# A cross network's first layer: the remainder of x0 in two loads, and the layer as x0 * (psum + b + 1)

## The chip, the core and the metric

The kernel runs on one core of one Trainium2 chip. The metric is the device time of one execution in microseconds (us), the median of several runs; lower is better. A profiled execution gives, beside it, a trace of every engine: TensorE (PE in the profile, its weight loads PEld), VectorE (DVE), ScalarE (ACT), GpSimd (POOL) and SyncE (SP), which here only issues DMAs. ACTq and SPq are the issuing sequencers of those engines.

## What is computed

```
B, F, D, L = 4096, 26, 16, 6
Din = min(F * D, 1024)            # 416
# x0: (4096, 416), ws: (6, 416, 416), bs: (6, 416), all bfloat16
x = x0
for l in range(6):
    x = x0 * (x @ ws[l] + bs[l]) + x
return x
```

In the first layer x is x0 itself, so that layer is x0 * (x0 @ w + b) + x0, which is the same as x0 * (x0 @ w + b + 1).

## The kernel before, in words

The work is held transposed: the 416 features lie on partitions and the 4096 rows of the batch are columns. The features are cut into NK = 3 blocks of 128 and a remainder of R = 32. The columns are cut into NS = 2 halves (s) of NG = 4 groups (g) of CW = 512. XM[0] holds x0's three blocks, XM[1] and XM[2] alternate as the layers' results; XR[0] to XR[2] hold the remainder, with group g of a half on partitions 32g to 32g+31. XRd is a second copy of x0's remainder with the two pairs of groups swapped (partitions 64 to 127 hold groups 0 and 1), so that two row matmuls can use different parts of the array.

*Loads.* `load_x0t(s, g)` (L74) loads one group of x0 with a transposing DMA, 393 KB, issued by SP. The remainder's 32 columns come as 64-byte pieces: for the first half by four DMAs on ACT's queue into xrig (L78), for the second by one on SP into xrem (L83), which POOL then regroups into xrig (L134). `load_wm` loads a layer's weights for the three blocks, `load_wr0` (L87) the 32 remaining weight rows of layer 0, which ACT (twice) and POOL (once) copy to the other three groups of 32 partitions (L107 to L112). SP's issues stand in the order in which they are written: x0's groups 0 and 1, WR of layer 0, groups 2 and 3, group 0 of the second half, xrem, groups 1 to 3 of the second half, then the other layers' weights and row copies for the last layer.

*Fillers.* While the first loads are under way TensorE runs matmuls on a constant tile (`pe_filler`, L139): two of 256 columns, then nine of 512. Then it transposes the biases (`bias_setup`, L146), which DVE copies to bM and bR.

*First layer* (`first_layer`, L208), half by half. `full` (L211) is three 128 x 512 matmuls, one per feature block, for one output block m and one group; `row` (L217) adds the remainder's 32 rows to two groups; `mm_rem` (L191) makes the remainder's own output. PSUM has four buffers of two banks that are taken in turn, so a tile of two groups can start only when the fourth tile before it has been read out. `x0_rem` (L155) transposes xrig with four TensorE transposes into PSUM and has DVE copy the result to XR[0] (one copy of 128 partitions) and XRd (two of 64). In the first half the order on TensorE is: group 0 for all m, x0_rem for the first half, group 1 for all m, rows, groups 2 and 3 of m = 0, 1, 2, rows, mm_rem, x0_rem for the second half. `ew_main` (L162) follows for each tile: ACT adds the bias while it reads PSUM (L165), DVE multiplies with x0 (L166), DVE adds the old x (L169). `ew_rem` (L171) does so for the remainder.

*Layers 1 to 4* (L282) work in the same transposed form with matmuls cut into four column tiles (L181), and the last layer is made row by row (L315 onward) with the result sent out from there.

The order of instructions on an engine is a scheduler's, starting from the order in which they are written; `keep_in_program_order` pins one. A tile's readers and writers on different engines are kept apart by semaphores that the framework puts in; two engines that read one PSUM tile are also put one behind the other.

Of the kernel before, what the change touches and what calls it, by code (L numbers as in the profile page):

```python
# [9 lines left out]
ACT = mybir.ActivationFunctionType  # L10
ALU = mybir.AluOpType
BF16 = mybir.dt.bfloat16
FP32 = mybir.dt.float32
# [3 lines left out]
def kernel(  # L17
# [7 lines left out]
    nc = tc.nc  # L25
    B, D = x0.shape
    L = ws.shape[0]
    P = 128
    NK = 3
    R = D - NK * P  # L30
    assert R == 32 and B == 4096 and D == 416 and L >= 2
    NS = 2
    NG = 4
    CW = 512
# [5 lines left out]
    big = ctx.enter_context(tc.tile_pool(name="big", bufs=1))  # L40
    tpool = ctx.enter_context(tc.tile_pool(name="tpool", bufs=6))
# [3 lines left out]
    x0_v = x0.rearrange("(bt p) d -> p bt d", p=P)  # L45
# [13 lines left out]
    X0rows = big.tile([P, NBT, D], BF16)  # L59
    XLrows = big.tile([P, NBT, D], BF16)  # L60
    scrR = [big.tile([P, 4, P], BF16, name=f"scrR{s}") for s in range(NS)]
    xrem = big.tile([P, 16, R], BF16)
    xrig = big.tile([P, NS, 4, P], BF16)
    XRd = big.tile([P, NS * CW], BF16)
    XM = [big.tile([P, NK, B], BF16, name=f"XM{i}") for i in range(3)]
    XR = [big.tile([P, NS * CW], BF16, name=f"XR{i}") for i in range(3)]
# [1 line left out]
    def col0(s, g):  # L68
        return SW * s + CW * g
# [4 lines left out]
    def load_x0t(s, g):  # L74
        c0 = col0(s, g)
        nc.sync.dma_start_transpose(out=XM[0][:, :, c0:c0 + CW], in_=x0[c0:c0 + CW, 0:NK * P])  # L76

    def load_xrem0():  # L78
        with nc.allow_non_contiguous_dma(reason="64B row segments"):
            for i in range(4):  # L80
                nc.scalar.dma_start(xrig[:, 0, i, :].rearrange("p (g r) -> p g r", g=NG), x0_v[:, i:16:4, NK * P:D])

    def load_xrem1():  # L83
        with nc.allow_non_contiguous_dma(reason="64B row segments"):
            nc.sync.dma_start(xrem[:], x0_v[:, 16:32, NK * P:D])

    def load_wr0():  # L87
        nc.sync.dma_start(WR[0:R, 0, :], ws[0, NK * P:D, :])

    def load_wr(eng, g, l0, l1):  # L90
        eng.dma_start(WR[32 * g:32 * g + 32, l0:l1, :], ws[l0:l1, NK * P:D, :].rearrange("l r n -> r l n"))
# [8 lines left out]
    load_x0t(0, 0)  # L100
    load_wm(nc.scalar, 0)
    nc.scalar.dma_start(bsb[:], bs[:, :])
    load_x0t(0, 1)
    load_xrem0()
    load_wr0()
    nc.scalar.activation(dz[:, 1:2], dz[:, 0:1], ACT.Identity, bias=dz[:, 0:1], scale=1.0)  # L106
    for g in range(1, NG):  # L107
        dst, src = WR[32 * g:32 * g + 32, 0, :], WR[0:R, 0, :]
# [3 lines left out]
            nc.gpsimd.tensor_copy(dst, src)  # L112
    for g in range(2, NG):
        load_x0t(0, g)
    load_x0t(1, 0)
    load_xrem1()
    for g in range(1, NG):
        load_x0t(1, g)
    load_wm(nc.sync, 1)
    for g in range(NG):  # L120
# [10 lines left out]
            nc.gpsimd.tensor_copy(WD[32 * g:32 * g + 32, l0:l1, g, :], WR[32 * g:32 * g + 32, l0:l1, NK * P:D])  # L131

    fill_wd(0, 1)
    nc.gpsimd.tensor_copy(xrig[:, 1].rearrange("p i (g r) -> p i g r", g=NG), xrem[:].rearrange("p (g i) r -> p i g r", g=NG))  # L134
    fill_wd(1, L)

    wps = psum.tile([P, CW], FP32, tag="ps", name="wps")
# [1 line left out]
    def pe_filler(n, cols):  # L139
        for i in range(n):  # L140
            nc.tensor.matmul(wps[:, 0:cols], lhsT=warm[:, 0:P], rhs=warm[:, 0:cols], start=True, stop=True)  # L141

    pe_filler(2, 2 * P)
    pe_filler(8, CW)

    def bias_setup():  # L146
        pb = psum.tile([P, 4, 8], BF16, tag="ps", name="pb")
        for m in range(NK):
            nc.tensor.transpose(pb[:, m, 0:L], bsb[0:L, 128 * m:128 * m + 128], ident[0:L, 0:L])
        for g in range(NG):  # L150
            nc.tensor.transpose(pb[32 * g:32 * g + 32, 3, 0:L], bsb[0:L, NK * P:D], ident[0:L, 0:L], tile_position=(0, 32 * g))  # L151
        nc.vector.tensor_copy(bM[:], pb[:, 0:NK, 0:L])  # L152
        nc.vector.tensor_copy(bR[:], pb[:, 3, 0:L])

    def x0_rem(s, tpr):  # L155
        for i in range(4):
            nc.tensor.transpose(tpr[:, 128 * i:128 * i + 128], xrig[:, s, i, :], ident[:])  # L157
        for dst, src in ((slice(0, P), slice(0, P)), (slice(64, P), slice(0, 64)), (slice(0, 64), slice(64, P))):
            to = XR[0] if dst == src else XRd
            nc.vector.tensor_copy(to[dst, CW * s:CW * s + CW], tpr[src])  # L160

    def ew_main(l, s, m, h, pt, cur, nxt, pin=False):  # L162
        c0 = col0(s, 2 * h)
        t = tpool.tile([P, 2 * CW], BF16, name="t")
        nc.scalar.activation(t[:], pt[:].rearrange("p a b -> p (a b)"), ACT.Identity, bias=bM[:, m, l:l + 1], scale=1.0)  # L165
        prod = nc.vector.tensor_tensor(out=t[:], in0=t[:], in1=XM[0][:, m, c0:c0 + 2 * CW], op=ALU.mult)  # L166
        if pin:
            tc.keep_in_program_order(prod)
        nc.vector.tensor_tensor(out=nxt[:, m, c0:c0 + 2 * CW], in0=t[:], in1=cur[:, m, c0:c0 + 2 * CW], op=ALU.add)  # L169

    def ew_rem(l, s, pr, curR, nxtR):  # L171
# [34 lines left out]
                                    in_=nxt[:, k, SW * s:SW * s + SW])  # L206

    def first_layer(s):  # L208
        cur, curR, nxt, nxtR = XM[0], XR[0], XM[1], XR[1]

        def full(pt, m, h, gl, after_row):  # L211
            c0 = col0(s, 2 * h + gl)
            for k in range(NK):
                nc.tensor.matmul(pt[:, gl, :], lhsT=WM[:, 0, k, 128 * m:128 * m + 128], rhs=cur[:, k, c0:c0 + CW],  # L214
                                 start=(k == 0 and not after_row), stop=(k == NK - 1 and after_row))

        def row(pt, m, h, opens):  # L217
            for gl in range(2):
                rg = 32 * ((2 * h + gl) ^ (2 if m == 1 else 0))
                src = XRd if m == 1 else curR  # L220
                nc.tensor.matmul(pt[:, gl, :], lhsT=WR[rg:rg + 32, 0, 128 * m:128 * m + 128],  # L221
                                 rhs=src[rg:rg + 32, CW * s:CW * s + CW],
                                 start=opens, stop=not opens, tile_position=(rg, 0))

        def ph(m):
            return psum.tile([P, 2, CW], FP32, tag="ps", name=f"ph{m}")

        pa = [ph(m) for m in range(NK)]
        if s == 0:
            for m in range(NK):  # L230
                full(pa[m], m, 0, 0, False)
            tp0 = psum.tile([P, CW], BF16, tag="ps", name="tpr")
            x0_rem(0, tp0[:])
            for m in range(NK):
                full(pa[m], m, 0, 1, False)
        else:
            for m in range(NK):
                for gl in range(2):
                    full(pa[m], m, 0, gl, False)
        pb = [ph(0)]  # L240
        row(pa[0], 0, 0, False)
        row(pb[0], 0, 1, True)
        row(pa[2], 2, 0, False)
        row(pa[1], 1, 0, False)
        for m in range(NK):
            ew_main(0, s, m, 0, pa[m], cur, nxt)
        for m in range(NK):
            if m:
                pb.append(ph(m))
            for gl in range(2):  # L250
                full(pb[m], m, 1, gl, m == 0)
        row(pb[1], 1, 1, False)
        row(pb[2], 2, 1, False)
        pr = psum.tile([P, 2, CW], FP32, tag="ps", name="pr")
        mm_rem(0, s, pr[:, 0, :], cur, curR)
        if s == 0:
            x0_rem(1, pr[:, 1, :].bitcast(BF16)[:, 0:CW])
        for m in range(NK):
            ew_main(0, s, m, 1, pb[m], cur, nxt, pin=(s == 0))
        ew_rem(0, s, pr[:, 0, :], curR, nxtR)  # L260

    bias_setup()
    pe_filler(1, CW)
# [51 lines left out]
    l = LL  # L315
# [97 lines left out]
```

## Time and profile before

| | |
|---|---|
| device time, median of 3 runs | 130.6 us (130.56 to 130.76) |
| span of the profiled execution (first to last instruction) | 128.9 us |
| median less span | 1.7 us |
| busy: PE, DVE, ACT, POOL | 123.1, 107.1, 86.9, 5.9 us |
| first full matmul of the first layer (L214) starts | 5.84 us |
| first matmul of layer 1 (L181) starts | 26.73 us |
| DMA engines | in nine tenths or more of slices 2 to 12 of 40 |

The profiled execution's own device time is not given apart from its span; the runs' median stands beside it. A matmul in the trace is pipelined: 379 ns is the length of one, but the next can start 216 ns behind it, so TensorE's progress is read from starts, not from lengths. The chain of waits follows the end back to what released each step; an engine that is not on it is idle without cost. In a line of groups the numbers behind the bar are busy time and the mean of one, then the idle time ahead of the group with what ended it.

### The profile page before, as it was taken

What the parts mean: (1) busy time and instruction counts of PE and PEld (TensorE: products, weight loads), DVE (VectorE), ACT (ScalarE), POOL (GpSimd) and SP (SyncE); (2) the same over time, 40 slices, a digit from 0 to 9 for tenths busy, and PEclk for the clock granted to TensorE, in tenths of its full rate; (3) what the DMA queues carried; (4) which work ended last, traced back from release to release, by engine and by line L of the source; (5) the groups of instructions that cost most, each with busy time, mean ns of one, the idle gap of its engine ahead of it and who ended that gap; (6) DMA issues with size and microseconds to landing.
All of it is one profiled execution on the core that took longest, in us unless ns stands there. A gap on an engine that the chain in (4) does not pass through costs nothing.

```text
span 128.9 us, 3973 instructions
## 1 busy us (share of the span) xinstructions
PE 123.1 (96%) x1690; PEld 54.9 (43%) x1690; DVE 107.1 (83%) x197; ACT 86.9 (67%) x99; POOL 5.9 (5%) x18
## 2 busy tenths in 40 slices
PE   6999999999999999999999999999999999999960
PEld 2343443354444444444444444444444445445420
DVE  1032979999999898989898989898989899898991
ACT  0426783987848577848668848668847896569670
POOL 4022200600000000000000000000000000000000
PEclk9999999999999999999999999999999999999999
DMA  3999999999990000000000000000297999995754
GB/s 106 237 203 217 170 158 260 247 328 333 336 299 11 5 0 8 0 0 5 0 5 0 5 0 5 0 5 0 42 166 164 123 219 178 187 323 188 231 179 139
DMA packets 42102, 16.37 MB, mean 127 GB/s; under 512 B 30906, under 2 KB 42084, under 8 KB 42084
## 3 DMA queue, kind: packets, MB, share of 16 engines
q1 hardware_dynamic: 39416, 15.56, 54.6%
q10 hardware_dynamic: 2668, 0.56, 2.3%
q8 instruction: 13, 0.21, 0.7%
q14 instruction: 5, 0.04, 0.1%
HBM read 6.15 MB, written 3.41 MB: 74 GB/s over the span
## 4 chain that ended last, share of the span: by engine, by line
PE 80%; DMA 8%; DVE 5%; issue 2%; SPq 1%; ACT 1%; DVEq 0%
PE pt L181 49%; PE ph L214 9%; DMA XM<-in_x_dram 8%; PE py L327 8%; PE pt L187 5%; PE pr L198 5%; DVE t L355 3%; DVE o L344 2%; PE pr L193 2%; SPq L76 1%; PE py L333 1%; PE ph L221 1%; PE py L336 1%; ACT t L354 1%; PE pr L157 0%
## 5 line engine op out<-in xcount | busy, mean ns | idle before, releaser
L181 PE MATMUL pt<-XM,WM 128*32 128x512 bf16 x1152 | 65.2, 379 | 0.0
L165 ACT ACTIVATE t<-pt,bM 128x1024 bf16<-128x1024 f32 x48 | 49.6, 1115 | 18.3 <-PE pt L187 18.3
L166 DVE TENSOR_TENSOR t<-t,XM 128x1024 bf16<-128x1024 bf16 x60 | 41.4, 690 | 5.3 <-ACT t L165 5.3
L169 DVE TENSOR_TENSOR XM<-t,XM 128x1024 bf16<-128x1024 bf16 x60 | 41.8, 696 | 3.4
L181 PEld LDWEIGHTS <-WM 128*32 128x32 bf16 x1152 | 29.7, 97 | 33.8 <-issue 5.1
L354 ACT CAST t<-py 128x416 bf16<-128x416 f32 (+1 forms) x23 | 14.8, 642 | 4.8 <-PE py L327 2.1
L327 PE MATMUL py<-WM,XM 128*128 128x416 bf16 x96 | 17.7, 340 | 0.0
L214 PE MATMUL ph<-XM,WM 128*128 128x512 bf16 x72 | 16.5, 379 | 0.1
L165 ACT ACTIVATE t<-ph,bM 128x1024 bf16<-128x1024 f32 x12 | 12.5, 1114 | 4.4 <-PE ph L221 4.4
L327 PEld LDWEIGHTS <-XM 128*128 128x128 bf16 x96 | 9.0, 98 | 8.5 <-issue 1.4
L355 DVE TENSOR_TENSOR t<-t,X0rows 128x416 bf16<-128x416 bf16 (+1 forms) x23 | 10.4, 454 | 1.2 <-ACT t L354 1.2
L214 PEld LDWEIGHTS <-WM 128*128 128x128 bf16 x72 | 6.8, 98 | 8.6 <-issue 1.3
L344 DVE TENSOR_TENSOR o<-t,XLrows 128x416 bf16<-128x416 bf16 (+1 forms) x23 | 10.3, 451 | 0.0
L173 ACT ACTIVATE t<-pr,bR 128x512 bf16<-128x512 f32 x10 | 6.4, 684 | 2.7 <-PE pr L198 2.1
L198 PE MATMUL pr<-XM,WM 128*32 128x512 bf16 x120 | 8.2, 379 | 0.0
L187 PE MATMUL pt<-XR,WR 32*128 32x512 bf16 x96 | 7.3, 379 | 0.0
L141 PE MATMUL wps<-warm 128*128 128x512 bf16 (+1 forms) x11 | 4.4, 593 | 1.2 <-DVE warm L94 1.2
L175 DVE TENSOR_TENSOR XR<-t,XR 128x512 bf16<-128x512 bf16 x10 | 4.2, 423 | 0.7
L198 PEld LDWEIGHTS <-WM 128*32 128x32 bf16 x120 | 3.2, 97 | 3.1
L106 ACT ACT_TABLE_LOAD x1 | 1.3, 1283 | 4.3 <-DMA WM<-in_ws_dram 4.3
L174 DVE TENSOR_TENSOR t<-t,XR 128x512 bf16<-128x512 bf16 x10 | 4.2, 418 | 0.0
L152 DVE CAST bM<-pb 128x18 f32<-128x18 bf16 x1 | 0.2, 177 | 4.6 <-PE pb L151 4.6
(39 smaller groups left out, 33.6 us busy)
## 6 DMA issues: line engine op xcount, KB each, us to landing
X0rows<-in_x_dram SPq DMA_DIRECT2D x4, 832.0 KB, 11.6
out_dram<-o SPq DMA_DIRECT2D x9, 208.0 KB, 2.4
WM<-in_ws_dram SPq DMA_DIRECT2D x5, 312.0 KB
out_dram<-o SPq DMA_DIRECT2D x13, 104.0 KB, 1.7
WR<-in_ws_dram SPq DMA_DIRECT2D x4, 130.0 KB, 4.1
WM<-in_ws_dram ACTq DMA_DIRECT2D x1, 312.0 KB
XM<-in_x_dram SPq DMA_TRANSPOSE x8, 4.9
xrig<-in_x_dram ACTq DMA_DIRECT2D x4, 32.0 KB, 4.1
```

The source lines that it names most:

```text
L165: nc.scalar.activation(t[:], pt[:].rearrange("p a b -> p (a b)"), ACT.Identity, bias=bM[:, m, l:l + 1], scale=1.0)
L166: prod = nc.vector.tensor_tensor(out=t[:], in0=t[:], in1=XM[0][:, m, c0:c0 + 2 * CW], op=ALU.mult)
L169: nc.vector.tensor_tensor(out=nxt[:, m, c0:c0 + 2 * CW], in0=t[:], in1=cur[:, m, c0:c0 + 2 * CW], op=ALU.add)
L173: nc.scalar.activation(tr[:, 0:CW], pr, ACT.Identity, bias=bR[:, l:l + 1], scale=1.0)
L181: nc.tensor.matmul(pts[g // 2][32 * q:32 * q + 32, g % 2, :], lhsT=WM[:, l, k, 128 * m + 32 * q:128 * m + 32 * q + 32], rhs=cur[:, k, c0:c ...
L187: nc.tensor.matmul(pts[g // 2][:, g % 2, :], lhsT=WR[32 * g:32 * g + 32, l, 128 * m:128 * m + 128], rhs=curR[32 * g:32 * g + 32, CW * s:CW ...
L198: nc.tensor.matmul(pr[32 * g:32 * g + 32, :], lhsT=WM[:, l, k, NK * P:D], rhs=cur[:, k, c0:c0 + CW], start=False, stop=(k == NK - 1), tile ...
L214: nc.tensor.matmul(pt[:, gl, :], lhsT=WM[:, 0, k, 128 * m:128 * m + 128], rhs=cur[:, k, c0:c0 + CW], start=(k == 0 and not after_row), sto ...
L327: nc.tensor.matmul(py[:, 0:D], lhsT=cur[:, k, q_cols(q, g)], rhs=WM[:, l, k, :], start=((not closes) and k == 0), stop=(closes and k == NK ...
L344: tc.keep_in_program_order(nc.vector.tensor_tensor(out=o, in0=t, in1=xl, op=ALU.add))
L354: nc.scalar.copy(tv, src)
L355: tc.keep_in_program_order(nc.vector.tensor_tensor(out=tv, in0=tv, in1=X0rows[:, b, :], op=ALU.mult))
```

## The change

The remainder of the first half is loaded in two parts (a half's groups 0 and 1, then 2 and 3), all by SP; the four DMAs on ACT's queue go and WR of layer 0 takes their place. Each part has two TensorE transposes and four copies, two by ACT (to XR[0]) and two by DVE (to XRd). The second half's remainder comes in four DMAs straight into xrig, so POOL no longer regroups, and its transposes move from the end of the first half into the second. Groups are worked one at a time. The first layer is x0 * (psum + b + 1): bM and bR get 1.0 added for layer 0, block m = 1 is done by one DVE instruction that reads PSUM, blocks 0 and 2 by ACT and one DVE multiplication, and the addition of x0 is gone. One filler less runs.

```diff
-    xrem = big.tile([P, 16, R], BF16)
-    xrig = big.tile([P, NS, 4, P], BF16)
+    xrh = big.tile([P, 2, 4, 2, R], BF16)
+    xrig = big.tile([P, 4, P], BF16)
...
-    def load_xrem0():
+    def load_xrem0(h):
+        with nc.allow_non_contiguous_dma(reason="64B row segments"):
+            for g in range(2):
+                b0 = 4 * (2 * h + g)
+                nc.sync.dma_start(xrh[:, h, :, g, :], x0_v[:, b0:b0 + 4, NK * P:D])
+
+    def load_xrem1():
         with nc.allow_non_contiguous_dma(reason="64B row segments"):
             for i in range(4):
-                nc.scalar.dma_start(xrig[:, 0, i, :].rearrange("p (g r) -> p g r", g=NG), x0_v[:, i:16:4, NK * P:D])
...
+                nc.sync.dma_start(xrig[:, i, :].rearrange("p (g r) -> p g r", g=NG), x0_v[:, 16 + i:32:4, NK * P:D])
...
     nc.scalar.dma_start(bsb[:], bs[:, :])
+    load_wr0()
     load_x0t(0, 1)
-    load_xrem0()
-    load_wr0()
+    load_xrem0(0)
...
     for g in range(2, NG):
         load_x0t(0, g)
-    load_x0t(1, 0)
+    load_xrem0(1)
+    for g in range(2):
+        load_x0t(1, g)
     load_xrem1()
-    for g in range(1, NG):
+    for g in range(2, NG):
         load_x0t(1, g)
...
-    nc.gpsimd.tensor_copy(xrig[:, 1].rearrange("p i (g r) -> p i g r", g=NG), xrem[:].rearrange("p (g i) r -> p i g r", g=NG))
...
-    pe_filler(8, CW)
+    pe_filler(7, CW)
...
+        nc.vector.tensor_scalar_add(bM[:, :, 0:1], bM[:, :, 0:1], 1.0)
+        nc.vector.tensor_scalar_add(bR[:, 0:1], bR[:, 0:1], 1.0)
...
+    def x0_rem0(h, tp):
+        for j in range(2):
+            nc.tensor.transpose(tp[:, P * j:P * j + P], xrh[:, h, 2 * j:2 * j + 2].rearrange("p i g r -> p (i g r)"), ident[:])
+        for i in range(2):
+            src = tp[64 * i:64 * i + 64, 0:2 * P].rearrange("p (j c) -> p j c", j=2)
+            for to, at, put in ((XR[0], 64 * h, nc.scalar.copy), (XRd, 64 - 64 * h, nc.vector.tensor_copy)):
+                pin(put(to[at:at + 64, 0:CW].rearrange("p (j i c) -> p i j c", j=2, i=2)[:, i], src))
+
+    def x0_rem1(tp):
+        for i in range(4):
+            nc.tensor.transpose(tp[:, P * i:P * i + P], xrig[:, i, :], ident[:])
+        pin(nc.vector.tensor_copy(XR[0][:, CW:2 * CW], tp))
+        pin(nc.scalar.copy(XRd[64:P, CW:2 * CW], tp[0:64]))
+        pin(nc.vector.tensor_copy(XRd[0:64, CW:2 * CW], tp[64:P]))
+
+    def ew_first(s, m, h, pt, on_dve):
+        c0 = col0(s, 2 * h)
+        src, x, b = pt[:].rearrange("p a b -> p (a b)"), XM[0][:, m, c0:c0 + 2 * CW], bM[:, m, 0:1]
+        nxt = XM[1][:, m, c0:c0 + 2 * CW]
+        if on_dve:
+            pin(nc.vector.scalar_tensor_tensor(out=nxt, in0=src, scalar=b, in1=x, op0=ALU.add, op1=ALU.mult))
+            return
+        t = tpool.tile([P, 2 * CW], BF16, name="t")
+        pin(nc.scalar.activation(t[:], src, ACT.Identity, bias=b, scale=1.0))
+        pin(nc.vector.tensor_tensor(out=nxt, in0=t[:], in1=x, op=ALU.mult))
...
         pa = [ph(f"pa{m}") for m in range(NK)]
+        for m in range(NK):
+            full(pa[m], m, 0)
+        full(pa[0], 0, 1)
+        full(pa[1], 1, 1)
+        pb = [ph("pb0")]
         if s == 0:
+            x0_rem0(0, as_bf16(pb[0][:, 0, :]))
         else:
+            x0_rem1(as_bf16(pb[0][:, 1, :]))
+        full(pa[2], 2, 1)
+        row(pa[0], 0, 0)
+        row(pa[1], 1, 0)
+        row(pa[2], 2, 0)
+        if s == 1:
+            row(pb[0], 0, 1, True)
+        for m in (1, 0, 2):
+            ew_first(s, m, 0, pa[m], m == 1)
+        full(pb[0], 0, 2, s == 1)
+        pb += [ph("pb1"), ph("pb2")]
+        full(pb[1], 1, 2)
+        full(pb[2], 2, 2)
+        pr = ph("pr")
+        if s == 0:
+            x0_rem0(1, as_bf16(pr[:, 1, :]))
         for m in range(NK):
+            full(pb[m], m, 3, s == 1 and m == 0)
+        if s == 0:
+            row(pb[0], 0, 1)
+        row(pb[1], 1, 1)
+        row(pb[2], 2, 1)
         mm_rem(0, s, pr[:, 0, :], cur, curR)
+        for m in (1, 0, 2):
+            ew_first(s, m, 1, pb[m], m == 1)
+        ew_first_rem(s, pr[:, 0, :])
```

## Prediction

> **What bounds the kernel now.** I read the page first, then the chain of waits in order of time, then TensorE's timeline in the head, then the groups by shape for prices. The page's chain says who sets the end, and the chain in order of time says where that begins:
>
> ```profile
> span 128.9 us, 3973 instructions
> PE 80%; DMA 8%; DVE 5%; issue 2%; SPq 1%; ACT 1%; DVEq 0%
> ```
>
> ```profile
> 0.74 4.86 DMA XM<-in_x_dram
> 5.61 1.44 SPq L76
> 7.10 5.00 DMA XM<-in_x_dram
> 12.14 3.40 PE ph L214 x15
> ...
> 26.90 2.59 PE pt L181 x48
> ```
>
> Loads set the pace until 12.14 us; from there to 115.8 us the chain is TensorE matmuls without a break, and the last ten microseconds are the drain of the results. So DVE and ACT work taken out of the first layer is worth nothing by itself: only TensorE stalls in the head count, and every one that is added is paid in full, since no idle TensorE time follows that could take it up. TensorE's timeline of the head (start, length, instructions) shows the stalls of today:
>
> ```profile
> 4.57 1.06 PE L141 MATMUL wps<-warm 128*128 128x512 bf16 x2
> 5.84 2.12 PE L214 MATMUL ph<-XM,WM 128*128 128x512 bf16 x9
> 7.80 0.81 PE L157 MATMUL tpr<-ident,xrig 128*128 128x128 bf16 x4
> 8.62 2.10 PE L214 MATMUL ph<-XM,WM 128*128 128x512 bf16 x9
> 10.66 0.60 PE L221 MATMUL ph<-XR,WR 32*128 32x512 bf16 x6
> ...
> 17.01 4.05 PE L214 MATMUL ph<-XM,WM 128*128 128x512 bf16 x18
> ```
>
> ```profile
> 11.20 1.32 PE L214 MATMUL ph<-XM,WM 128*128 128x512 bf16 x4
> ```
>
> A full matmul takes 379 ns but starts every 0.216 us (18 of them in the chain's 3.88 us from 17.18). Nine that start at 5.84 are issued by 7.78; the next nine start at 8.62. Between lie four transposes that cost 0.055 each when fed (0.22 from 16.78 to 17.01), so 0.62 is a stall. Nine from 8.62 end at 10.56 and the rows of L221 start at 10.66: 0.1. Four matmuls from 11.20 that take 1.32 instead of 1.03 hold a wait of 0.29 for the fourth column group.
>
> **Why 8.62.** The second transposed load is the slow one: issued at 2.16, and the longest of L76's "DMA to landing" is 6.4 us, so it lands near 8.6.
>
> ```profile
> 2.16 2.56 SPq L76 DMA_TRANSPOSE XM<-in_x_dram  x1
> DMA to landing us min/median/max: 4.3/4.9/6.4
> ```
>
> Its packets share the 16 DMA engines with 2048 packets of 64 bytes (the four xrig loads). The first load landed at 5.60.
>
> **What goes.** (a) One filler less (0.43 us) ends the fillers at 5.0, so the bias transposes run before the first load lands at 5.60; full work can start at about 5.65 instead of 5.84: -0.2. (b) The four xrig loads leave the ACT queue. In the trace they put about 1.1 us of DMA-engine time among the second load's packets; without them it should land between 7.0 and 7.6, about when nine matmuls from 5.65 end (7.59): -0.62. (c) WR's first load moves from SP to ACT's queue, behind bsb; its two ACT copies (0.54 each) then run before ACT has anything else to do: -0.1. (d) The fourth group is needed only after nine matmuls of the third, near 13.5, where it lands near 12.1 today; on SP the two xrh issues (0.4 to 0.6 each, from xrig and xrem) stand where WR's stood, and g2 no longer waits for g0's landing: -0.29. Together -1.2. The transposes stay eight in all.
>
> **What comes.** T is the start of the two new transposes: 5.65 + 15 x 0.216 = 8.9.
>
> (e) The copies of the first half's remainder. Today three DVE copies of 0.42 lie under nine matmuls (1.94 us). In the change the cover is three matmuls of pa2, 0.65. The order of instructions shows four copies in a strict relay: ACT, DVE, ACT, DVE, each waiting for the one before, because both engines read one PSUM tile. Rows for the prices:
>
> ```profile
> L173 ACT ACTIVATE t<-pr,bR 128x512 bf16<-128x512 f32 x2 | 1.4, 687 | 0.6 <-DVE XRd L160 0.6
> L165 ACT ACTIVATE t<-ph,bM 128x1024 bf16<-128x1024 f32 x12 | 12.5, 1114 | 4.4 <-PE ph L221 4.4
> L160 DVE COPY XRd<-tpr 64x512 bf16<-64x512 bf16 x2 | 0.8, 422 | 0.0
> L152 DVE CAST bM<-pb 128x18 f32<-128x18 bf16 x1 | 0.2, 177 | 4.6 <-PE pb L151 4.6
> ```
>
> ACT: 1114 - 687 = 427 ns for 512 more elements, so some 0.26 fixed and 0.44 to 0.47 for 256 elements; I take 0.44. DVE: between 0.18 (18 elements) and 0.42 (512), so 0.28 for 256. Hand-overs in this trace are 0.04 (ACT to DVE) to 0.09 (DVE to ACT). From T: second transpose done 0.27, start 0.30, ACT 0.74, DVE 1.07, ACT 1.59, rows of pa0 at 1.65; second DVE copy done 1.92, rows of pa1 at 1.98. TensorE is free at 0.11 + 0.65 = 0.76 and works 0.13 between the two: stall 1.1. Bounds: with every copy at its fixed part (0.25, 0.15) and no hand-over 0.2; with 0.69 and 0.42 it is 1.9.
>
> The Trainium skill's PSUM page ("PSUM — Partial Sum Buffer", section "PSUM bank collisions raise a hardware error") says that ScalarE and VectorE must not read one bank in the same 32-partition quadrant at once, so such reads have to be put one behind the other. By it the relay can't be shortened by luck; no run here shows a collision. Without the rule one would count only the longer engine, about 0.9, and get a stall of 0.6.
>
> (f) pb1 takes pa0's PSUM buffer. pa0's rows start at T+1.65; ACT starts 0.43 behind a first row (21.00 to 21.43 in the trace), so 2.08, and with 1.11 the buffer is free at 3.25. TensorE gets there at 1.98 + 0.3 + 0.65 = 2.93: stall 0.3 (0.2 to 0.45). pa1's fused DVE instruction on PSUM has no row; between one bf16 pass (0.69) and two (1.4) it ends by 3.85, and pb2 needs the buffer at 3.9: nothing. (g) In the second half pa0 needs pb0's buffer: pb0's rows at X, free at X+0.43+1.11+0.06 = X+1.6; TensorE arrives after six rows (0.43) and the remainder (0.98) at X+1.4: 0.2 (0 to 0.3). (h) In the second half xrig's transposes move under three matmuls as well. DVE copy 0.42, then ACT's of XRd: 0.38 + 0.03 + 0.42 + 0.05 + 0.69 + 0.06 = 1.63 after the first transpose; TensorE is there at 0.22 + 0.65 + 0.2 = 1.1: 0.55 (0 to 0.55). Today POOL's regrouping and all three DVE copies were hidden. The xrh1 relay lies under nine matmuls and costs nothing; without that cover it would be another 1.9.
>
> Loads: xrh1, s1's groups and four xrig issues instead of one xrem keep SP some 2 to 3 us longer, so layer 1's WM, issued at 17.97 and landed near 22.3 today, lands near 25 and is needed near 27.5. Hidden by about 2 us. The multiply-only form takes 12 adds of 0.69 off DVE, and the two bias adds are tiny: off the chain.
>
> **Sum.** 1.1 + 0.3 + 0.2 + 0.55 = 2.15 against 1.2: +0.95, span 129.85. The runs' median, 130.6, lies 1.7 above the profiled span; with the same surround the forecast is 131.55. With all low ends the net is about -0.4, with all high ends +2.0.
>
> **Rivals.** *Short copies* (faster): if each relay copy takes only its fixed part, with no hand-over, (e) is 0.2, (h) 0, (f) 0.4, (g) 0.2: 0.8 against 1.2 gives 130.2. It turns once relay copies average under about 0.2. For it: no row here has a 256-element PSUM copy; against it: ACT's slope of 0.83 ns an element in two rows. Chance 0.11, and 0.06 for ending within 0.2% (0.26 us, about what a measurement can tell) on the way there.
>
> *Late xrh* (slower still): xrig's landings took a median 4.1 us and xrem's 4.3 from issue. xrh's second load is issued near 5.3; at 4.4 it lands at 9.7 instead of before 8.9, and the transposes stall TensorE 0.8 more: 132.35. Against it: xrem waited behind a transposed load, here too, but this one should have drained by 6.2. Chance 0.12.
>
> *Slow clock*: fillers start every 0.43 us, first-layer matmuls every 0.216; the slow step lasted from 1.19 to at least 5.43 (the page's granted clock has a 9 in every slice, the first too, so only the step tells). With the fillers ending at 5.0 the run is broken for some 0.5 us; if the slow step then lasted another 4.2 us from 5.65, ten matmuls would be done in place of nineteen: +2.1, 133.6. For: the same fillers led straight to the fast step. Against: the gap is short. Chance 0.05. The Trainium skill ("TensorE: Matmul & The Clock Gate", Part 1) has the gate judged in free-running windows of 3.4 us, so a missed window would cost about 1.7; the trace's two steps agree with its two clocks.
>
> **How the numbers follow.** Forecast (net +0.3 to +1.6) 0.66; the rivals 0.11 + 0.06, 0.12, 0.05. Range 130.5 to 132.5: it leaves out short copies at their best, the slow clock and the far ends of (e). Faster 0.11, same 0.06, slower 0.83.
>
> **What would show it.** (a, b) first full matmul near 5.65, ninth followed within 0.1 by the tenth. (e) a gap of about 1.1 between pa2's second-group matmuls and pa1's rows, with ACT, DVE, ACT, DVE end to end in it. (f) 0.3 before pb1. (g, h) 0.2 and 0.5 in the second half; layer 1 starting near 27.7 instead of 26.7. If layer 1 starts before 26.7 the prediction is wrong; if the tenth matmul waits past 8.0, (b) is.

## The result, and the profile after

The changed kernel takes 132.41 us (median of 4 runs, 131.93 to 132.63) against 130.68 for the kernel before in the same session (4 runs, 130.56 to 131.12): a ratio of 1.0121, 95% interval 1.0088 to 1.0154. It is slower by 1.2%, 1.6 us by the ratio. The forecast was 131.55 with a range of 130.5 to 132.5: the direction held, and the time lies at the range's upper end.

The profiled execution took 132.42. Its span and its shares by engine, from the page of after:

```profile
span 130.6 us, 3961 instructions
PE 82%; DVE 6%; DMA 4%; ACT 3%; issue 2%; DVEq 0%
```

Loads give up half of their share of the chain (8% to 4%) and ACT gains 2: the first layer now waits for copies instead of loads. The chain of waits of after, in order of time (start, length, what):

```profile
0.73 4.89 DMA XM<-in_x_dram
...
5.66 3.81 PE pa L245 x15
9.47 0.12 PE pb L165 x2
...
9.62 0.37 ACT XR L169
...
10.02 0.29 DVE XRd L169
...
10.34 0.38 ACT XR L169
...
10.76 0.41 PE pa L252 x2
...
28.28 2.59 PE pt L212 x48
```

The loads leave the chain at 5.6 us, where those of before held it until 12.1 (the head, in what follows, is everything ahead of layer 1). In their place stands the relay: the transposes end at 9.59, ACT copies, DVE copies, ACT copies, and 1.2 us later the rows of L252 start. TensorE's timeline of after (start, length, instructions, idle before) shows what that costs and where it comes again:

```profile
9.42 0.81 PE L245 MATMUL pa<-XM,WM 128*128 128x512 bf16 x3
10.76 0.39 PE L252 MATMUL pa<-XR,WR 32*128 32x512 bf16 x2 [0.52 <-ACT XR L169]
...
20.84 0.81 PE L245 MATMUL pa<-XM,WM 128*128 128x512 bf16 x3
21.59 0.60 PE L252 MATMUL pa<-XR,WR 32*128 32x512 bf16 x3
22.13 0.39 PE L252 MATMUL pa<-XRd,WR 32*128 32x512 bf16 x2
...
22.59 0.39 PE L252 MATMUL pb<-XR,WR 32*128 32x512 bf16 x2
```

Three matmuls are issued in 0.65 us, so TensorE is free at 10.06, but it starts the rows at 10.76. In the second half it is free at 21.49 and is done with its eight rows at 22.91; eight rows that are fed take 0.54 (the chain of before). Layer 1 starts at 28.11 instead of 26.73: 1.38 us of the profiled span's 1.62 (128.93 to 130.55).

**The other 0.25 us** lies behind the last instruction that computes. Both kernels end with ACT issuing the last output; it lands 1.73 us later in before and 1.74 in after. Then the end differs. SP waits for the DMA semaphores one after another. In before, the last output's is the last of these waits; in after it is the first of five, and the other four follow after it has landed, 0.06 each. The groups of SP's last line (instructions, duration in ns min/median/max), in before:

```profile
L408 SPq EVENT_SEMAPHORE  x7: 17/28/28, 126.4 to 128.9; - x7
```

and in after, where one wait takes the whole landing and the rest stand behind it:

```profile
L444 SPq EVENT_SEMAPHORE  x7: 17/28/1677, 127.8 to 130.5; - x7
```

From the last issue to the end it is 2.57 us before and 2.82 after. Before has 64 DMA issues, after 67.

### The profile page after: what moved, and what is told of

It is laid out like the page before. It is cut to its first block, busy times and chain, and to the rows that moved or that the text cites. A ratio compares the mean times of both kernels' runs of the same rounds, so it can differ in the third digit from the quotient of the medians.

```text
span 130.6 us, 3961 instructions
## 1 busy us (share of the span) xinstructions
PE 123.9 (95%) x1689; PEld 55.3 (42%) x1689; DVE 100.4 (77%) x185; ACT 84.8 (65%) x100; POOL 4.1 (3%) x17
## 4 chain that ended last, share of the span: by engine, by line
PE 82%; DVE 6%; DMA 4%; ACT 3%; issue 2%; DVEq 0%
PE pt L212 49%; PE py L363 8%; PE pb L245 6%; PE pa L245 6%; PE pt L218 5%; PE pr L229 5%; DMA XM<-in_x_dram 4%; DVE t L391 3%; DVE o L380 2%; PE pr L224 2%; PE pb L252 1%; PE py L369 1%; ACT t L186 1%; PE py L372 1%; ACT t L390 1%
## 5 line engine op out<-in xcount | busy, mean ns | idle before, releaser
L199 DVE TENSOR_TENSOR t<-t,XM 128x1024 bf16<-128x1024 bf16 x48 | 32.9, 686 | 5.8 <-ACT t L198 5.8
L200 DVE TENSOR_TENSOR XM<-t,XM 128x1024 bf16<-128x1024 bf16 x48 | 33.2, 692 | 3.1
L245 PE MATMUL pa<-XM,WM 128*128 128x512 bf16 x36 | 8.8, 393 | 0.2 <-DMA XM<-in_x_dram 0.2
L245 PE MATMUL pb<-XM,WM 128*128 128x512 bf16 x36 | 8.4, 380 | 0.1
L186 ACT ACTIVATE t<-pb,bM 128x1024 bf16<-128x1024 f32 x4 | 4.3, 1112 | 3.3 <-PE pb L252 1.8
L204 ACT ACTIVATE t<-pr,bR 128x512 bf16<-128x512 f32 x8 | 5.1, 683 | 2.1 <-PE pr L229 2.1
L187 DVE TENSOR_TENSOR XM<-t,XM 128x1024 bf16<-128x1024 bf16 x8 | 5.2, 684 | 0.2 <-ACT t L186 0.2
L183 DVE SCALAR_TENSOR_TENSOR XM<-pb,bM,XM 128x1024 bf16<-128x1024 f32 x2 | 2.6, 1284 | 3.2 <-PE pb L252 3.2
L186 ACT ACTIVATE t<-pa,bM 128x1024 bf16<-128x1024 f32 x4 | 4.2, 1110 | 0.5 <-PE pa L252 0.5
```

Source lines behind the costliest of these rows:

```text
L186: pin(nc.scalar.activation(t[:], src, ACT.Identity, bias=b, scale=1.0))
L245: nc.tensor.matmul(pt[:, g % 2, :], lhsT=WM[:, 0, k, 128 * m:128 * m + 128], rhs=cur[:, k, c0:c0 + CW], start=(k == 0 and not after_row), ...
```

## The experiments

One table for all twelve. The ratio is to runs of the kernel before on the same chip in the same session. "Profiled" is the profiled execution's own time; layer 1's start and the tail (last output's issue to the end) are read from it, so a profile that lies off its median has to be read with that.

| kernel | median us | ratio, 95% interval | profiled | layer 1 starts | tail |
|---|---|---|---|---|---|
| before | 130.68 | | | 26.73 | 2.57 |
| after | 132.41 | 1.0121 (1.0088 to 1.0154) | 132.42 | 28.11 | 2.82 |
| e1_filler | 132.32 | 1.0117 (1.0086 to 1.0147) | 132.44 | 28.09 | 2.82 |
| e2_all_dve | 131.98 | 1.0093 (1.0064 to 1.0123) | 131.93 | 27.70 | 2.81 |
| e3_cover | 132.39 | 1.0114 (1.0073 to 1.0154) | 132.52 | 28.20 | 2.83 |
| e4_half2 | 131.88 | 1.0081 (1.0049 to 1.0112) | 132.41 | 28.07 | 2.81 |
| e5_evac | 132.43 | 1.0109 (1.0085 to 1.0134) | 132.26 | 27.95 | 2.82 |
| e6_form | 134.71 | 1.0282 (1.0254 to 1.0310) | 134.74 | 30.29 | 3.01 |
| e8_xrh_act | 132.68 | 1.0128 (1.0100 to 1.0156) | 133.03 | 28.76 | 2.83 |
| c1_combined | 131.66 | 1.0054 (1.0034 to 1.0075) | 131.97 | 27.82 | 2.74 |
| e9_before_form | 130.90 | 1.0006 (0.9984 to 1.0029) | 130.54 | 26.55 | 2.57 |
| e10_relay | 131.78 | 1.0067 (1.0047 to 1.0087) | 131.35 | 27.10 | 2.82 |
| c2_xrem | 131.27 | 1.0039 (1.0021 to 1.0058) | 131.30 | 27.33 | 2.56 |
| c3_early | 131.21 | 1.0020 (1.0003 to 1.0037) | 131.11 | 27.12 | 2.56 |

### e1_filler: the ninth filler back

In after, the first matmuls of the layer still ran at the slow step: 15 of them took 3.65 us (5.66 to the transposes at 9.31), not 15 x 0.216 = 3.24. Is the missing filler the cause?

```diff
-    pe_filler(7, CW)
+    pe_filler(8, CW)
```

> The change with the removed filler put back (eight of 512 columns instead of seven), nothing else. In the changed kernel's trace the 15 matmuls from 5.66 us took 3.65 us instead of 3.24, because they began at the slow step (0.43 us). Theory 'filler': the gap that the missing filler leaves keeps the clock slow, so with it back the 15 take 3.24, the first full matmul starts near 5.84, and the time falls by 0.2 to 0.25 us, to about 132.2. Theory 'phase': when the fast step comes is not set by one filler more or less; then the slow step can reach into the first matmuls here too, the first full matmul just starts 0.2 later, and the time is 132.3 to 132.7.

The 15 matmuls took 3.25 us and the first rows started at 10.28 instead of 10.76, yet layer 1 started at 28.09 against 28.11. The timeline of e1 shows what took the gain:

```profile
13.62 0.27 PE L165 MATMUL pr<-ident,xrh 128*128 128x128 bf16 x2 [0.29 <-DMA xrh<-in_x_dram]
```

The transposes of xrh's second part ran at 13.64 in after; here TensorE is there earlier, waits for the load, and runs them at 13.62. From these transposes to layer 1 it is 14.47 us in after, in e1 alike, and 14.46 in e2 and e3. So the load sits close under the first half, and terms of the head before 13.6 us don't add up freely. A single profile fixes its landing (the last of the DMA's semaphore updates in the trace) only loosely: it was 13.35 in after, 13.48 in e1 and 12.69 in e2, and 12.69 to 13.78 in the nine kernels that issue the first half's loads in this order. Whether the filler decides the clock is answered by all profiles together: the step to the full rate, in the trace's record of the clock, came at 4.59 to 6.57 us in the fourteen kernels, at 4.99 with nine fillers here, 5.63 in before (nine), 6.53 in after and 4.59 in e3 and e10 (eight). It isn't the filler.

### e2_all_dve: no relay in the first half

All four copies on DVE, XR[0]'s two first.

```diff
-        for i in range(2):
-            src = ...
-            for to, at, put in ((XR[0], 64 * h, nc.scalar.copy), (XRd, 64 - 64 * h, nc.vector.tensor_copy)):
+        for to, at, put in ((XR[0], 64 * h, nc.vector.tensor_copy), (XRd, 64 - 64 * h, nc.vector.tensor_copy)):
+            for i in range(2):
+                src = ...
```

> The change, with all four copies of each part of the first half's remainder on DVE, those to XR[0] first. Theory 'relay' (the stall of 0.88 us behind pa2's second group is the chain of four copies that hand over between ACT and DVE): four DVE copies of 0.28 with no hand-over end 0.3 earlier and XR[0]'s two are done 0.55 earlier, so the rows of pa0 wait only some 0.2 and those of pa1 0.4 more; the stall falls from 0.88 to about 0.55 and the time by 0.3, to 132.1. Theory 'load' (the stall is WR's load or a late x0 load): no change, 132.4.

131.98 us; layer 1 0.4 earlier than in after. The timeline of e2:

```profile
9.36 0.81 PE L245 MATMUL pa<-XM,WM 128*128 128x512 bf16 x3
9.56 0.59 DVE L169 COPY XR<-pb 64x256 bf16<-64x256 bf16 x2 [3.57 <-PE pb L165]
10.18 0.59 DVE L169 COPY XRd<-pb 64x256 bf16<-64x256 bf16 x2
10.20 0.59 PE L252 MATMUL pa<-XR,WR 32*128 32x512 bf16 x3
...
10.83 0.39 PE L252 MATMUL pa<-XRd,WR 32*128 32x512 bf16 x2
```

Two things help, and the edit doesn't separate them. One engine in a row is faster than two in turns: the four copies take 1.21 us from first to last (9.56 to 10.77) instead of 1.41 (9.62 to 11.03). And XR[0] comes first: it is complete at 10.15 after two copies of 0.29, where the relay had three copies ahead of it. The rows start 0.84 behind the start of the three matmuls instead of 1.34. The relay is real, and worth 0.4 us here.

### e3_cover: six matmuls over the copies instead of three

```diff
         full(pa[0], 0, 1)
-        full(pa[1], 1, 1)
+        if s == 1:
+            full(pa[1], 1, 1)
...
             x0_rem0(0, as_bf16(pb[0][:, 0, :]))
+            full(pa[1], 1, 1)
```

> The change, with the first half's first two transposes three matmuls earlier, ahead of pa1's second group instead of behind it. Theory 'relay': the copies start 0.65 us earlier against the same work, the stall of 0.88 falls to about 0.25 and the time to 131.8. Theory 'load': the transposes or the rows then wait for their load instead, and the time stays at 132.4.

The stall at the first rows is nearly gone, and the time is unchanged (132.39): the wait moved to the loads. The timeline of e3:

```profile
10.83 2.10 PE L245 MATMUL pb<-XM,WM 128*128 128x512 bf16 x8 [0.53 <-DMA XM<-in_x_dram]
13.74 0.27 PE L165 MATMUL pr<-ident,xrh 128*128 128x128 bf16 x2 [0.80 <-DMA xrh<-in_x_dram]
```

The stall at the copies, 0.9 us in after, was covered by matmuls here and nothing came of it; e2 had 0.4 of it. The loads set what can be had. (In e3's profile they also landed late: group 2 at 10.79 against 10.24 in after, xrh's second part at 13.60. How much of that is the edit's doing one profile can't say.)

### e4_half2: the second half's transposes six matmuls earlier

```diff
+        pb = [ph("pb0")]
+        if s == 1:
+            x0_rem1(as_bf16(pb[0][:, 1, :]))
         full(pa[0], 0, 1)
         full(pa[1], 1, 1)
-        pb = [ph("pb0")]
...
-        else:
-            x0_rem1(as_bf16(pb[0][:, 1, :]))
```

> The change, with the second half's four transposes directly behind the first column group (six matmuls earlier). Theory 'relay': its stall of 0.88 us (0.48 ahead of pa1's rows, 0.33 ahead of pb0's rows, which share the transposes' PSUM tile) goes, as the copies lie under nine matmuls; time 131.5 to 131.6. Rival 'load': xrig lands at 19.3 us in the changed kernel, and the transposes now come due at 19.3, so if the second half's loads are at the limit the stall only moves to the transposes; time above 132.

131.88 us, 0.5 less than after. In its profile all eight rows of the second half run without a gap (21.95 to 22.5); the profiled execution is the slowest of its five (132.41), with a load wait of 0.62 in the first half, so the size is taken from the median: the second half's relay is worth about 0.5.

### e5_evac: pb0's buffer, wanted earlier and filled first

```diff
         full(pb[0], 0, 2, s == 1)
+        full(pb[0], 0, 3, s == 1)
         pb += [ph("pb1"), ph("pb2")]
...
-        for m in range(NK):
-            full(pb[m], m, 3, s == 1 and m == 0)
+        full(pb[1], 1, 3)
+        full(pb[2], 2, 3)
```

> The change, with pb0's second group (the fourth column group) taken ahead of pb1 and pb2 in both halves, so that TensorE has three matmuls to do while ACT reads pa0 out of the buffer that pb1 takes. Theory 'release' (the 0.3 us ahead of pb1 is that buffer): the wait goes, but the fourth group is now due at 12.06, where it lands at 12.05 in the changed kernel's trace, and the second two transposes come 0.35 later with six matmuls of cover (1.29) in place of nine, of which rows need 1.78: net -0.1, 132.3. Theory 'load floor' (what the first half waits for is the landing of xrh's second part near 13.4, so TensorE's earlier waits cost next to nothing): also within 0.2 of 132.4, but with the transposes never waiting for their load. A gain of 0.3 or more speaks for 'release' as a cost of its own.

132.43: nothing. The three matmuls moved ahead cover ACT's reading of pa0, as meant, but they need group 3, and wait 0.28 us for it at 12.19: another stall changed into a load.

### e6_form: the changed order with the old arithmetic

```diff
-        nc.vector.tensor_scalar_add(bM[:, :, 0:1], bM[:, :, 0:1], 1.0)
-        nc.vector.tensor_scalar_add(bR[:, 0:1], bR[:, 0:1], 1.0)
...
-        for m in (1, 0, 2):
-            ew_first(s, m, 0, pa[m], m == 1)
+        for m in range(NK):
+            ew_main(0, s, m, 0, pa[m], cur, XM[1])
```

and the same for the second pair of groups and the remainder (`ew_rem`).

> The change, with the first layer's arithmetic of before: ACT adds the bias to every tile, DVE multiplies and adds x0, no 1.0 in the bias. Theory 'off the chain': DVE and ACT work of this layer isn't what TensorE waits for, except that ACT reads three tiles one after the other where DVE took one, so the second two transposes' buffer comes free 1.0 us later in the first half (about +0.4 to +0.8) and the time is 132.6 to 133.2. Rival 'fused read': the fused DVE instruction (1.28 us on PSUM) holds buffers longer than ACT would; then it is below 132.2.

134.71, 2.3 us above after (2.1 by the ratios): all theories fell short. The timeline of e6 (all engines) around the second relay:

```profile
16.21 0.28 DVE L167 COPY XRd<-pr 64x256 bf16<-64x256 bf16 x1
...
16.53 0.37 ACT L167 COPY XR<-pr 64x256 bf16<-64x256 bf16 x1 [1.65 <-DVE XRd L167]
...
16.95 0.39 PE L250 MATMUL pb<-XR,WR 32*128 32x512 bf16 x2 [0.96 <-ACT XR L167]
```

DVE runs six multiplications and additions without a break from 12.11 to 16.18, and the relay's copies stand behind them. ACT waits 1.65 for DVE, TensorE 0.96 for ACT. In this order DVE and ACT are no longer idle cover: every piece of their work in front of a copy can delay TensorE. (The edit also takes the blocks in the order 0, 1, 2 and leaves their instructions unpinned; the arithmetic was not tried apart from that.)

### e9_before_form: the old order with the new arithmetic

The kernel before with `ew_first`, `ew_first_rem` and the two bias additions, nothing else.

```diff
+        nc.vector.tensor_scalar_add(bM[:, :, 0:1], bM[:, :, 0:1], 1.0)
+        nc.vector.tensor_scalar_add(bR[:, 0:1], bR[:, 0:1], 1.0)
...
-        for m in range(NK):
-            ew_main(0, s, m, 0, pa[m], cur, nxt)
+        for m in (1, 0, 2):
+            ew_first(s, m, 0, pa[m], m == 1)
```

and so for the second pair of groups and the remainder.

> The kernel before with the change's arithmetic of the first layer alone: 1.0 added to layer 0's biases, block 1 by one fused DVE instruction that reads PSUM, blocks 0 and 2 by ACT and one DVE multiplication, the remainder likewise; loads, transposes, copies and TensorE's order as before. Theory 'off the chain' (in the order of before, TensorE doesn't wait for ACT or DVE in the head): layer 1 starts at 26.5 to 26.8 and the time is within 0.3 of the kernel before. Rival 'the form is worth its 2.3 us' (what e6_form lost by undoing it in the change): 128.5 to 129.5.

130.90 and a ratio of 1.0006 (0.9984 to 1.0029): no difference. The same arithmetic is worth 2.3 us in the one order and nothing in the other.

### e8_xrh_act: the four xrh loads on ACT's queue, as the loads were before

```diff
-                nc.sync.dma_start(xrh[:, h, :, g, :], x0_v[:, b0:b0 + 4, NK * P:D])
+                nc.scalar.dma_start(xrh[:, h, :, g, :], x0_v[:, b0:b0 + 4, NK * P:D])
...
     load_xrem0(0)
+    load_xrem0(1)
...
-    load_xrem0(1)
```

> The change, with the four loads of the first half's remainder issued on ACT's queue behind WR, not on SP's. Theory 'SP issue' (each pair of xrh issues takes SP 1.1 us, in which the DMA engines run dry and every later x0 load is late): the groups of x0 land 0.5 to 1.0 us earlier from the third on, the second two transposes don't wait for xrh, and layer 1 starts 0.2 to 0.4 earlier (27.7 to 27.9); time 131.9 to 132.2, the second half's stall of 0.88 being left. Theory 'bandwidth' (the same bytes on the same DMA engines): xrh's packets delay the second group instead, TensorE waits for it near 7.6, and the time is 132.4 or more.

132.68, not better than after. SP's loads of x0 now follow each other without a break, but TensorE waits for group 1 again. The timeline of e8:

```profile
8.67 1.46 PE L245 MATMUL pa<-XM,WM 128*128 128x512 bf16 x6 [0.48 <-DMA XM<-in_x_dram]
```

Group 1 landed at 8.63; in before, with as many packets of 64 bytes on ACT's queue (2048), at 8.58; in after, where the first 1024 of them are issued by SP from 4.94 on, at 7.02. That is the prediction's step (b), shown from both sides. The other end of the first half gains: its last load, group 3, landed at 11.55, where in after xrh's second part landed at 13.35.

### c1_combined: e2, e4 and e8 together, six matmuls over the first copies, xrem in one load again

Beside those edits the second half's remainder comes by one DMA and is regrouped on POOL, as before.

```diff
-            for i in range(4):
-                nc.sync.dma_start(xrig[:, i, :].rearrange("p (g r) -> p g r", g=NG), x0_v[:, 16 + i:32:4, NK * P:D])
+            nc.sync.dma_start(xrem[:], x0_v[:, 16:32, NK * P:D])
...
+    nc.gpsimd.tensor_copy(xrig[:].rearrange("p i (g r) -> p i g r", g=NG), xrem[:].rearrange("p (g i) r -> p i g r", g=NG))
```

> The change with four corrections at once: xrh's four loads on ACT's queue; the second half's remainder as one load that POOL regroups, as before; the first two transposes three matmuls earlier with all copies on DVE; the second half's transposes behind its first column group. If the stalls found (0.88 and 0.3 in the first half, 0.88 in the second, loads late by SP's issues) are all there is, TensorE goes through the first layer with 0.55 at pb1 and 0.2 at the half's turn, layer 1 starts near 26.0, and the time is 129.8 to 130.2, below both kernels. If SP's issues are not what makes loads late, the third and fourth groups land as in the change, layer 1 starts near 26.8, and the time is 130.6 to 131.0.

131.66: missed by 1.5 us, and 0.7 above the other theory's range too. Removing every copy stall at once brought 0.7. e8's part costs, as TensorE waits 0.75 for group 1 at 8.71. And a wait that c1's edits leave alone stands in both halves, 0.4 us each: pb1 takes the buffer that ACT still reads pa0 from. The timeline of c1:

```profile
12.46 1.46 PE L245 MATMUL pb<-XM,WM 128*128 128x512 bf16 x5 [0.24 <-ACT t L186]
...
23.29 3.40 PE L245 MATMUL pb<-XM,WM 128*128 128x512 bf16 x15 [0.23 <-ACT t L186]
```

The bracket holds only the time with no matmul in flight; the three matmuls ahead, from 11.39 and 22.24, are issued by 12.04 and 22.89. All loads of c1's first half had landed by 11.50, and its layer 1 still starts 1.1 us later than that of before (in a profile that lies 0.3 above the median).

### e10_relay: e2 and e4 together, loads as in after

> The change with two corrections together, those of e2_all_dve (all four copies on DVE) and e4_half2 (the second half's transposes behind its first column group); the loads as in the change. Theory 'load floor' (xrh's second part lands near 13.4 whatever TensorE does before it): TensorE waits 0.3 to 0.8 at the second two transposes, layer 1 starts 14.46 - 0.85 = 13.6 to 13.9 behind them, near 27.3, and the time is 131.3 to 131.6, still above the kernel before. Theory 'relay alone' (stalls by copies are all): the second two transposes start at 12.8, layer 1 at 26.4, and the time is 130.4 to 130.6.

131.78, 0.6 below after (0.7 by the ratios), where e2 and e4 alone bring 0.4 and 0.5. In the profile xrh's second part is waited for again (0.16 at 13.03). That the parts don't add in full is what a late load would do, but the difference is hardly clear of the runs' spread (131.35 to 131.84 here, 131.53 to 132.41 in e4).

### c2_xrem: e10, six matmuls over the first copies, xrem in one load

The edits are c1's without e8's.

> The change with all copies of the first half on DVE, its first two transposes three matmuls earlier, the second half's transposes behind its first column group, and the second half's remainder as one load that POOL regroups, as before, in place of four issues on SP; xrh's loads stay on SP behind the second column group. Theory 'SP issue': with 1.6 us of SP's issues gone, the second half's last two groups land as before (near 20 and 21.3), and no wait for a load is left in the second half; the first half still waits for the third group (near 10.4) and for xrh's second part (near 13.4): layer 1 starts near 27.1, time 131.1 to 131.3. Theory 'bandwidth': the second half's loads are as late as in the change and TensorE waits 0.2 to 0.6 in it: 131.4 to 131.8.

131.27, 0.5 below e10 (0.4 by the ratios). About half of it is the tail: 64 DMA issues again, and 2.56 us instead of 2.82 from the last issue to the end. The rest can't be found in the two profiles, since e10's is the fastest of its nine runs and starts layer 1 earlier (27.10) than c2's (27.33). In c2, xrh is still waited for (0.40 at 13.26), and pb1 waits for its buffer in the second half (0.4 at 22.80).

### c3_early: c2 with xrh's second part ahead of group 3

```diff
-    for g in range(2, NG):
-        load_x0t(0, g)
+    load_x0t(0, 2)
     load_xrem0(1)
+    load_x0t(0, 3)
```

> The kernel of c2_xrem, with the second part of xrh issued on SP ahead of x0's fourth column group instead of behind it. In c2_xrem TensorE was ready for the second two transposes at 12.8 and waited until 13.26 for that part, which landed near 13.2. Theory 'load floor, by SP's order': the part lands near 11.7, the transposes start at 12.8, and the fourth group, now landing near 12.9 to 13.2, makes TensorE wait 0 to 0.3 behind them: layer 1 starts 0.15 to 0.45 earlier than 27.33, time 130.8 to 131.1. Theory 'floor by bytes': what stands last in the first half's loads lands near 13.2 in any order and TensorE needs all of it: no change, 131.2 to 131.4.

131.21, ratio 1.0020 (1.0003 to 1.0037). xrh is there in time, and now group 3 isn't. The timeline of c3:

```profile
12.59 0.28 PE L165 MATMUL pr<-ident,xrh 128*128 128x128 bf16 x2
13.16 2.10 PE L245 MATMUL pb<-XM,WM 128*128 128x512 bf16 x9 [0.30 <-DMA XM<-in_x_dram]
```

Whichever of the two is issued last lands at 13.12 (group 3 was there at 12.1 in before). c3 is the fastest version found, though not clear of c2 (1.0021 to 1.0058), and still doesn't beat the kernel before.

## Why the prediction was right, and where its sum was off

The direction held for the reason given: stalls of TensorE behind copies with little cover, against load waits saved. The sum was +0.95; the profiled executions show +1.62. That the time still fell inside the range is owed in part to the range's width: the slow step (0.41) and the tail (0.25) were in no term of the sum. By its own steps:

- **(a)** First matmul at 5.66 instead of 5.84: -0.18, forecast -0.2.
- **(b)** The tenth matmul runs without a wait, group 1 landed at 7.02 (forecast 7.0 to 7.6): -0.62 as forecast, and e8 shows the cause. (The small packets' share of the DMA engines was taken as 1.1 us; summed over before's trace, the 2048 take 1.44 us of all 16 engines.) But it was not the whole gain it seemed: with the step to the full rate at 6.53, the 15 matmuls took 0.41 longer than at the full rate. The prediction had this as a rival that costs 2.1 or nothing; its small form was missing. e1 shows that those 0.41 are hardly felt at the end, since the load floor takes them up.
- **(c)** This reading was wrong. The 0.1 ahead of the rows is no wait for WR: the same 0.1 stands where full matmuls give way to rows elsewhere, with WR long there: in before the 18 from 17.01 are issued by 20.90 and the rows start at 21.00, in after nine from 13.75 by 15.69 and the rows at 15.79. The change gained nothing there. The same 0.1 is inside the 0.70 of (e) below, so the balance is not moved by it.
- **(d)** -0.29 as forecast; group 3 had landed by 12.05 and no matmul waited.
- **(e)** 0.70 ahead of the rows and 0.20 between them: 0.9, forecast 1.1. The order was right, the hand-overs and ACT's copies a little shorter. That the relay could not be shorter was too strong, though: in the prediction's own words the rule holds within one 32-partition quadrant, and ACT's second copy reads partitions 64 to 127 while DVE's first reads 0 to 63. What put ACT's start at 10.34 behind DVE's end at 10.30 is the framework's order of two readers of one tile. The groups of after (mean ns behind the busy time):

```profile
L169 ACT COPY XR<-pb 64x256 bf16<-64x256 bf16 x2 | 0.7, 366 | 3.0 <-PE pb L165 2.7 <-DVE XRd L169 0.3
L169 DVE COPY XRd<-pb 64x256 bf16<-64x256 bf16 x2 | 0.6, 289 | 4.5 <-ACT XR L169 4.5
```

ACT's 256 elements took 0.37 (taken: 0.44), DVE's 0.29 (0.28), ACT's single copy of 512 elements in the second half (L175) 0.58 (0.69).
- **(f), (g)** 0.29 and 0.19, forecast 0.3 and 0.2. The fused DVE instruction on PSUM took 1.28, inside the bounds, and nothing waited for it.
- **(h)** 0.88, forecast 0.55. This step failed in its working: it stopped at the second copy. pb0's rows write the PSUM tile that holds the transposes, so they wait for the third copy too; DVE's last (22.11 to 22.55) is followed at once by pb0's rows at 22.59.
- **The tail**: +0.25, not in the sum. The prediction counted the added DMAs as work for SP's queue and not for the waits at the program's end.

With these, 0.95 + 0.41 (clock) - 0.2 (e) + 0.33 (h) + 0.25 (tail) is 1.74, near the 1.62 measured. One bound was added up wrongly: with all low ends, (e) 0.2, (f) 0.2, (g) 0 and (h) 0, the net is -0.8, not -0.4, which is the sum for *short copies*.

Of the rivals, *short copies* fell: relay copies averaged 0.33. *Late xrh* fell for the first part, which landed 2.4 us after its issue (7.96, needed at 9.31). For the second part, whose landing the prediction never worked out, it was nearly true: it landed at 13.35, 0.3 before TensorE came. *Slow clock* came in its small form.

Two sentences of the prediction were too simple, and only the experiments showed it. "DVE and ACT work taken out of the first layer is worth nothing by itself" holds in the order of before (e9) and is wrong by 2.3 us in the changed one (e6), where copies for TensorE queue behind that work. And the terms were added as if each stall were free to go; e1, e3 and e5 take away 0.4, some 0.8 and 0.3 us of it, and get waits for x0's groups and xrh's second part in its place.

**Where the 1.6 us come from.** In after's own profile no load makes TensorE wait once the first layer has begun. TensorE loses 0.9 and 0.88 behind copies, 0.29 and 0.19 for buffers and 0.41 at the slow step, 2.67 in all. Against that stand the 1.01 of waits that the prediction counted in before and a start that is 0.18 earlier. That makes 1.48, where layer 1 starts 1.38 later; the tail adds 0.25.

The experiments don't give these stalls back at their length. Both relays together are worth about 0.6 (e10), the tail about 0.25 (c2), and c3 comes within 0.3 of the kernel before by the ratio (0.4 by the medians). What then remains, some 0.7, is a remainder and not a measurement, and the traces show two things in it. One is pb1's wait for its buffer, term (f) of the sum, which c1 and c2 still have, and which before's timeline of the head doesn't show. The other is the head's last load, at 13.35 in after and 13.12 in c2 and c3, whichever load it is, instead of 12.1; in c3 TensorE still waits 0.8 us for x0's groups, in three places.

For the late landing the profile suggests a reason: SP issues the four xrh loads between x0's, and meanwhile the DMA engines are fed less. Busy time of the engines in two stretches (the last two columns are the DMA share, which counts a packet's whole time where it starts and so can pass 1, and GB/s), before:

```profile
6.50:7.70 1.20, 1.20 (x7) 0.59 (x6) 0.00 (x0) 0.00 (x0) 0.00 (x0) 1.00 1.15 166
11.00:12.40 1.40, 1.28 (x13) 0.44 (x6) 0.16 (x1) 1.31 (x2) 0.00 (x0) 1.00 1.13 181
```

and after:

```profile
6.50:7.70 1.20, 1.20 (x7) 0.59 (x6) 0.00 (x0) 0.46 (x1) 0.82 (x5) 1.00 0.65 64
11.00:12.40 1.40, 1.29 (x10) 0.46 (x8) 0.92 (x2) 1.22 (x2) 0.00 (x0) 1.00 0.81 107
```

and e8, with the same four loads on ACT's queue:

```profile
6.50:7.70 1.20, 1.20 (x7) 0.59 (x6) 0.00 (x0) 1.19 (x2) 0.42 (x2) 1.00 1.41 207
11.00:12.40 1.40, 0.99 (x8) 0.40 (x8) 0.53 (x2) 0.92 (x2) 0.00 (x0) 1.00 1.19 260
```

There the first half's last load landed at 11.55, and at 11.50 in c1, which has them on ACT's queue too. So the small packets alone don't hold it until 13.1; that takes their issue by SP. On ACT's queue the price is group 1, at 8.63 and 8.67.

**Open**: how much of the later landing is the time of SP's four issues and how much their place among x0's loads; a version with one load for each part was not run. What pb1's wait for its buffer costs by itself, with every load there in time, was not tried: e5 covers it but runs into group 3. ACT and DVE reading different partitions of the tile at the same time was not tried either; the framework puts any two readers of one PSUM tile one behind the other. That the number of DMAs alone sets the tail was not tried by itself; it agrees in the nine kernels with 67 issues (2.81 to 2.83, e6 3.01) and the five with 64 (2.56 to 2.57, c1 2.74); in e6 and c1 ACT's last drain came late.

## What to carry to other kernels

Before splitting a copy over two engines that read one PSUM tile, lay the copies end to end with their hand-overs, count the matmuls that cover them, and follow every tile that shares that PSUM buffer to its last reader: one engine in a row, with the tile that is needed first copied first, was faster here than two in turns. A stall is only worth its length if the load behind it has landed, so work out the landing of every load of the stage, the last one above all, before adding up stalls. Count a new DMA three times: its issue on the queue it joins, its packets beside the next transfer, and its place in the waits at the program's end.

## What the hardware showed that was not expected

- **The end of a program depends on which semaphore the last DMA uses.** Four waits that come after it in SP's list cost 0.06 us each: 0.25 us of 132.
- **The step to the full rate came at 4.59 to 6.57 us** in fourteen profiled kernels whose TensorE work began at the same 1.2 us; matmuls of 512 columns start every 0.43 us ahead of it and every 0.216 behind. In the page's granted clock it can't be seen (a 9 in the first slices). The Trainium skill ("TensorE: Matmul & The Clock Gate", Part 1) says that the window in which activity is judged runs freely, so that the change's time varies with its phase; this case's traces agree that the time varies, but over 2 us, where the page gives plus or minus 0.5 us.
- **Small loads hold SP longer than their bytes suggest**: 0.49 to 0.58 us for each of the four xrh issues of 32 KB, and 0.58 for xrem's 128 KB in one, about as much for four times the data. With 2048 packets of 64 bytes issued beside it, x0's second transposing load landed at 8.58 to 8.68 us (four kernels) instead of 6.81 to 7.02 (ten).
